# Sums of the attention in one trip, right-hand pieces by VectorE, an early opening of the gate's second half, and an own bank for its sixth product

## The chip, the cores and the metric

One core of one Trainium2 chip. The time is the device time of one execution in microseconds (us), the median of several runs. All arrays are fp32, and the matmuls run as three products of high and low parts (type fp32r): high x high, high x low and low x high.

## The reference

A block with two sublayers over 2048 tokens of width 640: windowed attention with 32 heads of 20, then a gated MLP in which a 2048x2048 matrix mixes tokens.

```python
x = A_x                                  # 2048 x 640
n = layernorm(x)
q, k, v = split(n @ wqkv)                # 32 heads of 20
p = softmax(q @ k.T * 20 ** -0.5, where 0 <= i - j < 256)
h = x + (p @ v) @ wo
z = gelu(layernorm(h) @ w_in)            # 2048 x 1728
z1, z2 = z[:, :864], layernorm(z[:, 864:])
g = w_sp @ z2 + b_sp[:, None]            # w_sp 2048 x 2048
h2 = h + (z1 * g) @ w_out
```

## The kernel before

*Stages.* Tokens are 16 tiles of 128. The stages follow one another, and TensorE works through nearly all of them: norms and the projections to q, k and v; the attention, a loop of some 130 steps `s`; the projection by `wo` (about 460 to 550 us); z1 (to 640); z2 of tiles 0 to 7, and of tiles 8 and 12 ahead of their turn (to 697); the gate's first half, eight row pairs over columns 0 to 1023 of w_sp (to 831); z2 of the other tiles (831 to 867); the gate's second half, with the last product and the output (867 to 1127). Each engine runs its instructions in one fixed order, and what stands ahead of an instruction on its engine is ahead of it in time.

*What sets the order.* Within the attention, `proj_early(s)` issues preparations of the projection at numbered steps, and SyncE's order is fixed by hand. Elsewhere a scheduler orders each engine by its own estimate of times, starting from the order in which the code issues. From z1 on the work is a list `steps`, each a product on TensorE and then the reading of its PSUM bank; `at(n, f)` issues a preparation at step n, `n0` is the first step of a pair.

*End of the attention.* `ot` is the unnormalised output of a head group, read out of its PSUM bank `pv` and stored to `o_d` in DRAM; row DH = 20 of it holds the softmax sums. `inverse_sums(c)` loads the sums of 512 tokens into `inv` (128x128), inverts them and stores them to `r_d`, from where `load_rs` spreads them over 128 partitions into the end of the buffer `m1`. `load_o(j)` loads two token tiles into m1 by five loads, `norm_o` multiplies by the inverse, `split_o` makes the high part (on VectorE where its second argument is True, otherwise on ScalarE) and the low part in `xb`, and `proj_o` multiplies by wo into `wo_ps`; then VectorE adds the residual `xh` and takes the statistics `mvc`.

*The gate.* For w_sp and z2 a pair of row tiles (p, p + 8) and a pair of z2 tiles are taken as 2x2 blocks, and seven products stand for the eight of a plain block product (Strassen's scheme in Winograd's form). They run in the order B11, T1, T2, B22, T3, B21, T4. Each has pieces of w_sp on the left (buffer `aw`, seven places of 1024 columns, high and low part; raw values in `fx`, one sum in `tmp1`) and pieces of z2 on the right (`zc[k]`, k = 0 to 3; in names ze0 to ze11 and zl0 to zl15 by 7k + product). A high part is a copy on ScalarE (`hi`, line 707), a low part or a block's sum is a subtraction (`lo`, `plus`, `minus`, line 701) by VectorE, or by GpSimd (POOL in the profile) where `eng` says so. Products share two banks of PSUM per pair: B11 and T1 open them, and each product's `post` reads its bank before a later one goes on in it.

*Rows and z2.* `row0` to `row3` are tiles of 128x864 that hold the results of a z2 pair or of a gate pair; a gate pair of the first half is stored to `g_d` and loaded back in the second half. `z2_pair` makes gelu, the norm and, by `right_blocks`, the pieces; a pair with `ahead` is stored to `z2_d`, and `z2_ready` loads it again at the end of the first half, splits it and fills zc[0]. `hn_d` holds the normed h. `win2_prep` is a generator, advanced once a step from z1 on, that loads the five 128x864 blocks of w_in's second half and splits them.

## Time and profile before

| what | value |
|---|---|
| time, median of 3 runs | 1132.14 us (1131.96 to 1132.17) |
| the profiled execution's own time | 1129.15 us |
| its span in the profile | 1127.4 us |
| mean granted TensorE clock | 0.994 |
| HBM traffic over the span | 154 GB/s |

In the rows of the profile PE is TensorE's matmuls, PEld its weight loads, DVE VectorE, ACT ScalarE, POOL GpSimd, SPq the queue of SyncE, which issues most DMAs. A row of the timeline reads: start in us, duration, engine, line, operation, out<-in by the program's names without their numbers, partitions x elements and type, count, and in brackets the idle time of the engine just ahead with what ended it. The time of a profiled execution lies a little off the median, since each execution has its own.

### The profile page before, as it was taken

How to read it: one execution, taken by the hardware profiler on the slowest of the kernel's cores; microseconds unless marked ns; L12 is line 12 of the kernel's file. 1: busy time of each engine (PE TensorE's matmuls, PEld its weight loads, DVE VectorE, ACT ScalarE, POOL GpSimd, SP SyncE). 2: the span in 40 equal slices, each digit the busy share in tenths (PEclk: the TensorE clock that was granted, in tenths of full speed). 3: DMA queues.
4: the chain of work that ended last, by engine and by line, in shares of the span. 5: the costliest groups of instructions: out<-in, count | busy, mean ns of one | idle time of the engine just before them, and what ended most of it. 6: DMA issues, size and time to landing. Idle time of an engine off the chain costs nothing.

```text
span 1127.4 us, 27668 instructions
## 1 busy us (share of the span) xinstructions
PE 1094.3 (97%) x10667; PEld 979.1 (87%) x10667; DVE 729.4 (65%) x2047; ACT 563.0 (50%) x1197; POOL 338.0 (30%) x470
## 2 busy tenths in 40 slices
PE   9999999999999999999999999999999899999998
PEld 7998877668877776799989999999988799999998
DVE  6541113889999998599567578545548965465542
ACT  4334333259999989435756567333336522122210
POOL 3114444457777768312120254000025000000000
PEclk9999999999999999899999999999999899999999
DMA  7212665656666653688645412343251554344322
GB/s 257 76 32 99 177 210 177 211 192 204 205 205 192 220 159 116 199 267 291 235 147 196 157 47 61 114 138 114 90 168 55 183 183 141 127 136 147 98 76 78
DMA packets 84580, 174.26 MB, mean 155 GB/s; under 512 B 11152, under 2 KB 47504, under 8 KB 80528
## 3 DMA queue, kind: packets, MB, share of 16 engines
q1 hardware_dynamic: 82144, 167.24, 46.2%
q10 hardware_dynamic: 2304, 5.24, 1.2%
q8 instruction: 84, 1.38, 0.5%
q14 instruction: 48, 0.39, 0.1%
HBM read 114.89 MB, written 58.75 MB: 154 GB/s over the span
## 4 chain that ended last, share of the span: by engine, by line
PE 74%; DMA 7%; DVE 6%; issue 4%; POOL 3%; ACT 3%; SPq 2%; POOLq 0%; DVEq 0%; ACTq 0%
PE g L1059 22%; PE out_ps L1098 8%; PE pv L419 6%; PE zb L947 5%; PE bank L325 5%; PE bank L391 5%; PE qk L509 2%; PE qk L511 2%; PE qk L510 2%; PE wo_ps L93 2%; PE zx L895 2%; PE zv L895 1%; POOL sg L528 1%; DMA qk_d<-sg 1%; PE zy L895 1%
## 5 line engine op out<-in xcount | busy, mean ns | idle before, releaser
L394 ACT ACTIVATE pt<-bank 128x384 f32<-128x384 f32 (+2 forms) x512 | 200.5, 495 | 12.6 <-PE bank L391 7.5
L1059 PE MATMUL g<-zl,aw 128*128 128x432 f32 x768 | 172.0, 360 | 5.1 <-ACT zl L707 4.5
L707 ACT ACTIVATE aw<-fx 128x512 fp32r<-128x512 f32 (+3 forms) x160 | 92.7, 594 | 166.5 <-PE g L1059 104.8
L337 DVE CUSTOM_DVE_ANT_0 junk<-bank,strip 128x288 bf16<-128x288 f32 x392 | 157.7, 454 | 4.4 <-PE bank L325 2.9
L1059 PEld LDWEIGHTS g<-zl,aw 128*128 128x128 f32 x768 | 144.2, 189 | 12.7 <-ACT zl L707 5.1
L1059 PE MATMUL g<-ze,aw 128*128 128x432 f32 x576 | 135.8, 364 | 4.2 <-DVE row L701 2.4
L419 PE MATMUL pv<-pt,v_sb 128*32 128x192 f32 (+3 forms) x1984 | 128.3, 322 | 1.7 <-POOL pt L399 0.6
L701 DVE TENSOR_TENSOR aw<-fx,aw 128x512 fp32r<-128x512 f32 (+3 forms) x152 | 104.9, 699 | 35.0 <-ACT aw L707 34.6
L1059 PEld LDWEIGHTS g<-ze,aw 128*128 128x128 f32 x576 | 108.0, 190 | 11.7 <-ACT aw L707 3.0
L391 PE MATMUL bank<-slot 123*32 123x288 bf16 (+5 forms) x1536 | 107.2, 280 | 1.1 <-ACT pt L394 0.6
L396 POOL TENSOR_SCALAR_AFFINE_SELECT pt<-pt 128x512 f32<-128x512 f32 x128 | 82.3, 643 | 51.7 <-ACT pt L394 50.7
L1098 PE MATMUL out_ps<-wout,y_sp 128*128 128x320 f32 (+1 forms) x630 | 96.2, 309 | 0.4 <-ACT y_sp L134 0.4
L947 PE MATMUL zb<-win,aw 128*128 128x432 f32 x480 | 95.5, 359 | 0.0
L1098 PEld LDWEIGHTS out_ps<-wout,y_sp 128*128 128x128 f32 (+1 forms) x630 | 94.1, 188 | 1.3 <-ACT y_sp L134 0.7
L947 PEld LDWEIGHTS zb<-win,aw 128*128 128x128 f32 x480 | 89.9, 188 | 5.0 <-ACT aw L707 0.4
L325 PE MATMUL bank<-slot 120*32 120x288 bf16 (+2 forms) x1264 | 88.8, 283 | 3.1 <-issue 2.1
L525 DVE TENSOR_TENSOR rest<-qk,sg 128x512 f32<-128x512 f32 x40 | 27.7, 692 | 86.1 <-ACT sg L523 86.1
L399 POOL TENSOR_SCALAR_AFFINE_SELECT pt<-pt 128x512 f32<-128x512 f32 x112 | 73.9, 660 | 0.0
L701 DVE TENSOR_TENSOR row<-g,row 128x432 f32<-128x432 f32 x80 | 48.0, 603 | 31.4 <-PE g L1059 27.3
L419 PEld LDWEIGHTS pv<-pt,v_sb 128*32 128x32 f32 x1984 | 60.6, 110 | 8.6 <-issue 2.4
L391 PEld LDWEIGHTS <-slot 123*32 123x32 bf16 x1536 | 53.6, 96 | 16.6 <-issue 5.4
L528 POOL TENSOR_TENSOR sg<-rest,sg 128x512 bf16<-128x512 f32 x40 | 46.6, 1164 | 69.6 <-ACT sg L527 57.3
(190 smaller groups left out, 2161.4 us busy)
## 6 DMA issues: line engine op xcount, KB each, us to landing
fx<-wsp_in SPq DMA_DIRECT2D x32, 512.0 KB
slot<-qk_d SPq DMA_DIRECT2D x72, 200.0 KB
qk_d<-sg SPq DMA_DIRECT2D x32, 384.0 KB
slot<-qk_d SPq DMA_DIRECT2D x72, 160.0 KB
fx<-hn_d SPq DMA_DIRECT2D x32, 320.0 KB
o_d<-ot SPq DMA_DIRECT2D x64, 128.0 KB
z_d<-row SPq DMA_DIRECT2D x18, 432.0 KB
g_d<-row SPq DMA_DIRECT2D x16, 432.0 KB
```

The source lines that it names most:

```text
L325: nc.tensor.matmul(ps[32 * j:32 * j + 32, :n], part(st, half, 120, 0, hh, q0, 32), part(st, half, 120, 1, hh, lo + skip * j, n), start=Tru ...
L337: nc.vector.tensor_tensor_reduce(out=junk[:, :n], in0=ps[:, :n], in1=keep, scale=1.0, scalar=NEG, op0=OP.add, op1=OP.max, accum_out=m_cols ...
L391: nc.tensor.matmul(ps[32 * i:32 * i + 32, b:e], part(st, half, 123, 1, hh, k0, 32), part(st, half, 123, 0, hh, kb * P + b, e - b), start=T ...
L394: nc.scalar.activation(pt[:, hh, :n], ps[:, :n], AF.Exp, scale=SCALE)
L396: nc.gpsimd.affine_select(out=pt[:, :, :P], in_=pt[:, :, :P], pattern=[[0, 4], [1, P]], base=0, channel_multiplier=-1, compare_op=OP.is_ge ...
L399: nc.gpsimd.affine_select(out=pt[:, :, 256:], in_=pt[:, :, 256:], pattern=[[0, 4], [-1, P]], base=-1, channel_multiplier=1, compare_op=OP. ...
L419: nc.tensor.matmul(ps[32 * hh:32 * hh + 32, a - 512 * c:b - 512 * c], v_sb[:, kb, v0:v0 + 32], pt[:, hh, a - kb * P:b - kb * P], start=fir ...
L701: (eng or nc.vector).tensor_tensor(out=out, in0=a, in1=b, op=op)
L707: nc.scalar.activation(out, a, AF.Copy)
L947: nc.tensor.matmul(b[0][:, :HF], a[t][:, x, kk], win2[0][:, y, kk, h * HF:(h + 1) * HF], start=kk + x + y == 0, stop=kk == KD - 1 and x == 1)
L1059: nc.tensor.matmul(ps, w[m][:, x, k], zc[k][m][:, y], start=start and k + x + y == 0, stop=stop and k == 3 and x == 1, skip_group_check=True)
L1098: nc.tensor.matmul(ps[j][:, :HD], src[:w, a, k, :], e1["wout"][:w, b, k, j * HD:(j + 1) * HD], start=(k == 0 and a + b == 0), stop=(k == K ...
```

## The change

- `load_o` gives three functions. `load_sums` loads the sums of the first two tiles straight from o_d, spread over 128 partitions, and VectorE inverts them in place (128x256). This serves tiles 0 and 1; the others use r_d as before. The loads begin at step 117 instead of 118, the norms and splits of tiles 0 and 1 run at steps 122 to 125 instead of 125 to 127, and the high part of tile 2 is made by VectorE.
- `win2_prep` subtracts on VectorE, with five steps instead of four between load and copy and behind the subtraction.
- `z2_pair` of pairs 13 and 14 (q > 12) makes its pieces with VectorE alone, as pair 15 did.
- `z2_ready` loads into two row tiles instead of places of `fx`, at n0 - 5 and n0 - 4 instead of n0 - 9 and n0 - 8, and its first pieces come one or two steps later.
- `gate_pair`, second half: sums by VectorE in the first pair too (`p or c`). The first pair (`alone`) loads w_sp at n0 - 23 and makes the pieces of B11, T1, T2 at n0 - 17 to n0 - 14; B21 has its own place in aw and its own bank, opened by itself, and its pieces are made at n0 - 4 and n0 - 3; the second pair's preparations shift by one step. The order in which the code issues the products stays; the scheduler may put B21 elsewhere.
- The rows of the second half and the raw tile of w_out change names to match.

```diff
@@ load_o
-        for k in range(KD):
-            nc.sync.dma_start(ot[:, k], o_d[:, 4 * k:4 * k + 4, t])
+        def load_tiles():
+            for k in range(KD):
+                nc.sync.dma_start(ot[:, k], o_d[:, 4 * k:4 * k + 4, t])
...
+        def load_sums():
+            load_rs(o_d[:, DH, t], 32 * S)
+            return lambda: nc.vector.reciprocal(out=rs, in_=rs)
+
+        return load_tiles, load_rs, load_sums
@@ proj_early
-        if s == 118:
-            mem["rs"] = [load_o(0)]
+        if s == 117:
+            tiles, _, sums = load_o(0)
+            mem["invert"] = sums()
+            tiles()
         if s == 121:
-            mem["rs"][0]()
-            load_o(1)()
+            for f in load_o(1)[:2]:
+                f()
+            mem["invert"]()
+        if s == 122:
+            norm_o(0, nc.vector)
+        if s == 123:
+            split_o(0, True)
+        if s == 124:
+            norm_o(1, nc.vector)
         if s == 125:
-            norm_o(0, nc.vector)
+            split_o(1, True)
         if s == 126:
-            split_o(0, True)
...
         if s == 127:
...
-            norm_o(1, nc.vector)
-            split_o(1, True)
@@ win2_prep
-            for _ in range(4):
+            for _ in range(5):
...
-            minus(win2[0][:, 1, k], raw, win2[0][:, 0, k].bitcast(F32), nc.gpsimd)
-            for _ in range(4):
+            minus(win2[0][:, 1, k], raw, win2[0][:, 0, k].bitcast(F32))
+            for _ in range(5):
@@ z2_pair
-        f = right_blocks(lambda: zc[k], *blocks, nc.vector if k == 3 else nc.gpsimd)
+        f = right_blocks(lambda: zc[k], *blocks, nc.vector if k == 3 or q > 12 else nc.gpsimd)
@@ z2_ready
-        z = [view(fx, 2048 + t * FH, FH) for t in range(2)]
+        z = [row(), row()]
...
-            at(n0 - 9 + t, lambda t=t: nc.sync.dma_start(z[t], z2_d[t]))
-        for n, g in zip((-5, -4, -3, -1, 0, 0, 0), f):
+            at(n0 - 5 + t, lambda t=t: nc.sync.dma_start(z[t], z2_d[t]))
+        for n, g in zip((-3, -3, -2, -1, 0, 0, 0), f):
@@ gate_pair
+        alone = p == 0 and c == 1
+        if alone:
+            w[B21] = two(view(aw, 4608, 2, 4, P))
+            w[T3] = [view(aw, o, 4, P) for o in (4096, 5632)]
...
-        eng = nc.vector if p else nc.gpsimd
+        eng = nc.vector if p or c else nc.gpsimd
...
+        if p == 1 and c == 1:
+            preps[4:7] = [(-2, lambda: lo(T2, a11)), (-1, lambda: (hi(T3, a21), hi(B21, a12))),
+                          (0, lambda: (lo(T3, a21), s4(), hi(T4, a22)))]
...
-        at(n0 - 11 if p != 1 else n0 - 10, load)
+        if alone:
+            preps = [(-17, lambda: hi(B11, a11)), (-16, lambda: (lo(B11, a11), s13(), hi(T1, s1))),
+                     (-15, lambda: (s2(), lo(T1, s1), hi(T2, a11))), (-14, lambda: lo(T2, a11)),
+                     (-4, lambda: hi(B21, a12)), (-3, lambda: lo(B21, a12)), (-2, lambda: minus(a12, a12, a11)),
+                     (0, lambda: (hi(T3, a21), hi(T4, a22))), (1, lambda: (hi(B22, a12), lo(T3, a21))),
+                     (2, lambda: (lo(B22, a12), lo(T4, a22)))]
+        at(n0 - (10 if p == 1 else 23 if alone else 11), load)
...
-            if m in (B11, T1):
-                gbank[p, half] = bank("a", f"g{c}_{p}_{half}")
+            if m in (B11, T1) or m == B21 and alone:
+                gbank[p, half] = bank("b" if m == B21 else "a", f"g{c}_{p}_{half}_{m}")
@@ the loop of the projection
-            split_o(i + 1, False)
+            split_o(i + 1, i == 1)
```

In the orders below, the numbers behind the names only tell buffers apart. On VectorE at the end of the attention, before (`inv` and `r_d` carry the inverted sums, `ot7` and `pv7` the last head group, xb0 and xb1 the parts for the projection):

```order
L373 RECIPROCAL inv0_8951<-inv0_8951 128x128
L435 COPY ot7_1_0_9267<-pv7_1_9087 128x256
L435 COPY ot7_1_1_9270<-pv7_1_9087 128x256
L158 TENSOR_TENSOR m1_8946<-m1_8946 128x5x128
L164 CAST xb0_96<-m1_8946 128x640
L167 TENSOR_TENSOR xb0_96<-m1_8946,xb0_96 128x640
L158 TENSOR_TENSOR m1_8946<-m1_8946 128x5x128 x2
L373 RECIPROCAL inv1_8952<-inv1_8952 128x128
L158 TENSOR_TENSOR m1_8946<-m1_8946 128x5x128
L167 TENSOR_TENSOR xb1_97<-m1_8946,xb0_96 128x640
L164 CAST xb1_97<-m1_8946 128x640
```

and after:

```order
L384 RECIPROCAL inv0_8951<-inv0_8951 128x128
L446 COPY ot7_1_0_9268<-pv7_1_9087 128x256
L446 COPY ot7_1_1_9271<-pv7_1_9087 128x256
L157 RECIPROCAL m1_8946<-m1_8946 128x256
L163 TENSOR_TENSOR m1_8946<-m1_8946 128x5x128
L169 CAST xb0_96<-m1_8946 128x640
L172 TENSOR_TENSOR xb0_96<-m1_8946,xb0_96 128x640
L163 TENSOR_TENSOR m1_8946<-m1_8946 128x5x128
L169 CAST xb1_97<-m1_8946 128x640
L163 TENSOR_TENSOR m1_8946<-m1_8946 128x5x128 x2
L172 TENSOR_TENSOR xb1_97<-m1_8946,xb1_97 128x640
L384 RECIPROCAL inv1_8952<-inv1_8952 128x128
```

The 128x256 reciprocal in m1 is new; the norm, high and low parts of tile 0 and the high part of tile 1 (`CAST xb1`) now stand ahead of the norms of tiles 2 and 3 (`x2`), and the low part of tile 1 behind them. On SyncE, at the loads that feed these, before:

```order
L436 DMA o_d_66<-ot7_0_0_9124 128x256
L436 DMA o_d_66<-ot7_0_1_9127 128x256
L370 DMA inv0_8951<-o_d_66 128x1x128
L146 DMA m1_8946<-o_d_66 128x1x256 x5
L374 DMA r_d_67<-inv0_8951 32x4x128
L436 DMA o_d_66<-ot7_1_0_9267 128x256
L436 DMA o_d_66<-ot7_1_1_9270 128x256
L152 DMA m1_8946<-r_d_67 128x1x256
L146 DMA m1_8946<-o_d_66 128x1x256 x5
```

and after:

```order
L447 DMA o_d_66<-ot7_0_0_9124 128x256
L447 DMA o_d_66<-ot7_0_1_9127 128x256
L153 DMA m1_8946<-o_d_66 128x1x256
L147 DMA m1_8946<-o_d_66 128x1x256 x5
L381 DMA inv0_8951<-o_d_66 128x1x128
L385 DMA r_d_67<-inv0_8951 32x4x128
L447 DMA o_d_66<-ot7_1_0_9268 128x256
L447 DMA o_d_66<-ot7_1_1_9271 128x256
L147 DMA m1_8946<-o_d_66 128x1x256 x5
L153 DMA m1_8946<-r_d_67 128x1x256
```

The load of the sums takes the place of `inv`'s, which goes behind the five tile loads, and r_d's first load goes. On VectorE at the end of the gate's first half (`g0_7` is the last pair, row0 and row1 its result, `ze` the pieces of z2), before:

```order
L701 TENSOR_TENSOR ze4_10556<-fx_9613,ze4_10556 128x432
L701 TENSOR_TENSOR fx_9613<-fx_9613 128x512
L701 TENSOR_TENSOR row1_9608<-g0_7_0_12604,row1_9608 128x432
L701 TENSOR_TENSOR aw_9612<-fx_9613,aw_9612 128x512
L701 TENSOR_TENSOR ze3_10555<-fx_9613,ze3_10555 128x432
L701 TENSOR_TENSOR row0_9607<-g0_7_1_12621,row0_9607 128x432
L701 TENSOR_TENSOR aw_9612<-fx_9613,aw_9612 128x640
L701 TENSOR_TENSOR ze5_10557<-fx_9613,ze5_10557 128x432
```

and after:

```order
L712 TENSOR_TENSOR row1_9609<-g0_7_0_0_12605,row1_9609 128x432
L712 TENSOR_TENSOR aw_9613<-fx_9614,aw_9613 128x512
L712 TENSOR_TENSOR ze0_10553<-row2_9610,ze0_10553 128x432
L712 TENSOR_TENSOR row2_9610<-row2_9610 128x432
L712 TENSOR_TENSOR ze3_10556<-row3_9611,ze3_10556 128x432
L712 TENSOR_TENSOR row2_9610<-row3_9611,row2_9610 128x432
L712 TENSOR_TENSOR row0_9608<-g0_7_1_1_12622,row0_9608 128x432
L712 TENSOR_TENSOR aw_9613<-fx_9614,aw_9613 128x640
```

Before, one piece (`ze3`) stands between the readings of g0_7_0 into row1 and of g0_7_1 into row0; after, four rows that read the loaded row2 and row3 do. On SyncE the loads of z2 there, before:

```order
L1072 DMA g_d_71<-row0_9607 128x864
L999 DMA fx_9613<-z2_d_73 128x864 x2
L1073 DMA g_d_71<-row3_9610 128x864
L956 DMA fx_9613<-hn_d_70 128x640
L1072 DMA g_d_71<-row2_9609 128x864
L956 DMA fx_9613<-hn_d_70 128x640 x2
L1073 DMA g_d_71<-row1_9608 128x864
```

and after:

```order
L1097 DMA g_d_71<-row3_9611 128x864
L967 DMA fx_9614<-hn_d_70 128x640
L1010 DMA row3_9611<-z2_d_73 128x864
L1096 DMA g_d_71<-row2_9610 128x864
L1010 DMA row2_9610<-z2_d_73 128x864
L967 DMA fx_9614<-hn_d_70 128x640 x2
L1097 DMA g_d_71<-row1_9609 128x864
```

The loads from z2_d went behind the last pairs' stores, and row2's load directly follows the store out of row2. On TensorE at the opening of the gate's second half (`g1_0_0` and `g1_0_1` are the banks of the first pair), before:

```order
L1059 MATMUL g1_0_0_13073<-ze0_10552,aw_9612 128x432 x3
L1059 MATMUL g1_0_0_13073<-ze7_10559,aw_9612 128x432 x3
L1059 MATMUL g1_0_0_13073<-zl2_9593,aw_9612 128x432 x3
L1059 MATMUL g1_0_1_13100<-ze1_10553,aw_9612 128x432 x3
L1059 MATMUL g1_0_1_13100<-ze8_10560,aw_9612 128x432 x3
L1059 MATMUL g1_0_1_13100<-zl3_9594,aw_9612 128x432 x3
L1059 MATMUL g1_0_0_13073<-zl9_9600,aw_9612 128x432 x3
L1059 MATMUL g1_1_0_13216<-ze0_10552,aw_9612 128x432 x2
```

and after:

```order
L1083 MATMUL g1_0_0_0_13075<-ze0_10553,aw_9613 128x432 x3
L1083 MATMUL g1_0_0_0_13075<-ze7_10560,aw_9613 128x432 x3
L1083 MATMUL g1_0_0_0_13075<-zl2_9594,aw_9613 128x432 x3
L1083 MATMUL g1_0_1_1_13100<-ze1_10554,aw_9613 128x432 x3
L1083 MATMUL g1_0_1_1_13100<-ze8_10561,aw_9613 128x432 x3
L1083 MATMUL g1_0_1_1_13100<-zl3_9595,aw_9613 128x432 x3
L1083 MATMUL g1_0_1_5_13174<-ze5_10558,aw_9613 128x432 x3
L1083 MATMUL g1_0_1_5_13174<-zl0_9592,aw_9613 128x432 x3
L1083 MATMUL g1_0_1_5_13174<-zl7_9599,aw_9613 128x432 x3
L1083 MATMUL g1_0_0_0_13075<-zl9_9601,aw_9613 128x432 x3
L1083 MATMUL g1_0_1_5_13174<-zl14_9606,aw_9613 128x432
```

Nine matmuls of B21 (ze5, zl0, zl7, bank g1_0_1_5) now stand ahead of the first matmul with zl9, a piece made from the last z2 pair.

More of the change, by code (lines that the diff above doesn't have):

```diff
@@ L144, in load_o, with load_rs @@
         ot, rs = m1(j % 2 * 2 * D, KD, 2 * P), m1(6 * D + j % 2 * 2 * P, 2 * P)
-        for k in range(KD):
-            nc.sync.dma_start(ot[:, k], o_d[:, 4 * k:4 * k + 4, t])
+        def load_tiles():
+            for k in range(KD):
+                nc.sync.dma_start(ot[:, k], o_d[:, 4 * k:4 * k + 4, t])
         for i in range(2):
             ots[2 * j + i] = (ot[:, :, i * P:(i + 1) * P], rs[:, i * P:(i + 1) * P])
-        def load_rs():
-            base = r_d[:, t]
-            nc.sync.dma_start(rs, bass.AP(tensor=base.tensor, offset=base.offset, ap=[[S, H], [0, 4], [1, 2 * P]]))
-        return load_rs
+        def load_rs(base=r_d[:, t], step=S):
+            nc.sync.dma_start(rs, bass.AP(tensor=base.tensor, offset=base.offset, ap=[[step, H], [0, 4], [1, 2 * P]]))
+        def load_sums():
+            load_rs(o_d[:, DH, t], 32 * S)
+            return lambda: nc.vector.reciprocal(out=rs, in_=rs)
+        return load_tiles, load_rs, load_sums
     def norm_o(i, eng):
@@ L1013, in gate_pair @@
         s1 = view(tmp1, 0, 4, P)
-        w = [view(aw, m * 1024, 2, 4, P) for m in range(7)]
+        w = [two(view(aw, m * 1024, 2, 4, P)) for m in range(7)]
+        alone = p == 0 and c == 1
+        if alone:
+            w[B21] = two(view(aw, 4608, 2, 4, P))
+            w[T3] = [view(aw, o, 4, P) for o in (4096, 5632)]
         def load():
@@ L1018, in load @@
                 nc.sync.dma_start(view(fx, f0 + o, 8, P), wsp[t, :, 8 * c:8 * c + 8, :])
-        eng = nc.vector if p else nc.gpsimd
+        eng = nc.vector if p or c else nc.gpsimd
         def hi(m, raw):
-            copy(w[m][:, 0], raw)
+            copy(w[m][0], raw)
         def lo(m, raw):
-            minus(w[m][:, 1], raw, w[m][:, 0].bitcast(F32))
+            minus(w[m][1], raw, w[m][0].bitcast(F32))
         def s13():
@@ L1058, in prod @@
                 for x, y in ((0, 0), (0, 1), (1, 0)):
-                    nc.tensor.matmul(ps, w[m][:, x, k], zc[k][m][:, y], start=start and k + x + y == 0,
+                    nc.tensor.matmul(ps, w[m][x][:, k], zc[k][m][:, y], start=start and k + x + y == 0,
                                      stop=stop and k == 3 and x == 1, skip_group_check=True)
@@ L1118, in final_half @@
             nc.sync.dma_start(out[tile_of(n) * P:(tile_of(n) + 1) * P, c], ht[:, c])
-    gate_rows = (rows[n] for n in [0, 1] + [2, 0, 1] * 5)
+    gate_rows = (rows[n] for n in [2, 3] + [0, 2, 1] * 5)
     def second_gate(p):
@@ L1162, in wout_raw @@
             def wout_raw(k):
-                return e1["h"][0 if k < 4 else 1]
+                return e1["h"][0] if k < 4 else rows[1][:, :D]
             def load_wout(k):
@@ L1198, in block_kernel @@
         if 1 < i + 1 < NT:
-            split_o(i + 1, False)
+            split_o(i + 1, i == 1)
         if i % 2 == 0 and i + 4 < NT:
-            load_o(i // 2 + 2)()
+            for f in load_o(i // 2 + 2)[:2]:
+                f()
         if i + 2 < NT:
```

## Prediction

> **What bounds the kernel now.** I read the page's head first, then the waits of TensorE, then tables of windows around each wait, and last the timelines of the engines that end the waits.
>
> ```profile
> span 1127.4 us, 27668 instructions
> PE 1094.3 (97%) x10667; PEld 979.1 (87%) x10667; DVE 729.4 (65%) x2047; ACT 563.0 (50%) x1197; POOL 338.0 (30%) x470
> ```
>
> TensorE is busy for 97% of the span, so 33 us are all that edits of the other engines can win, plus what a lowered clock adds. The change removes no matmul. The question is which pieces of those 33 us it touches. The columns below are window, length, then busy time with count for PE, PEld, DVE, ACT and POOL, and the granted clock.
>
> ```profile
> 465.00:468.70 3.70, 1.59 (x21) 0.91 (x20) 3.61 (x6) 1.23 (x3) 0.59 (x1) 0.92 0.77 214
> 468.70:474.80 6.10, 6.03 (x22) 6.03 (x23) 2.85 (x8) 2.28 (x4) 0.55 (x1) 0.50 0.93 315
> 831.50:867.30 35.80, 35.76 (x182) 33.63 (x181) 25.46 (x46) 19.42 (x34) 18.06 (x15) 1.00 0.35 112
> 867.00:875.50 8.50, 3.98 (x21) 3.44 (x19) 8.29 (x14) 6.17 (x12) 5.81 (x6) 0.93 0.22 67
> 875.50:881.20 5.70, 4.79 (x11) 3.55 (x12) 4.63 (x10) 4.18 (x7) 0.46 (x1) 0.51 0.97 345
> 876.00:906.00 30.00, 27.75 (x127) 24.54 (x127) 28.06 (x49) 14.84 (x25) 0.00 (x0) 0.91 0.56 177
> ```
>
> Two places lose time. At the end of the attention TensorE idles 3.70 - 1.59 = 2.1 us, and then runs 6.03 us at clock 0.50, where full clock would need 3.0: together 5.1 us. At the opening of the gate's second half it idles 8.50 - 3.98 = 4.5 us and then 30.00 - 27.75 = 2.25 us, and 4.79 busy us run at clock 0.51, which costs 2.35 more: 9.1 us.
>
> **The change, part by part.**
>
> *End of the attention.* Here is who holds whom now.
>
> ```profile
> 449.71 0.95 DVE L373 RECIPROCAL inv<-inv 128x128 f32<-128x128 f32 x1 [1.31 <-DMA inv<-o_d]
> 450.58 0.69 DVE L435 COPY ot<-pv 128x256 f32<-128x256 f32 x2
> 462.00 1.56 DVE L158 TENSOR_TENSOR m<-m 128x640 f32<-128x640 f32 x2 [1.42 <-DMA m<-r_d]
> 466.19 0.81 DVE L164 CAST xb<-m 128x640 fp32r<-128x640 f32 x1
> 467.95 0.76 DVE L167 TENSOR_TENSOR xb<-m,xb 128x640 fp32r<-128x640 f32 x1
> 467.10 0.53 PE L93 MATMUL wo_ps<-xb,xb 128*128 128x320 f32 x2 [1.03 <-PE pv L419]
> 468.77 1.43 PE L93 MATMUL wo_ps<-xb,xb 128*128 128x320 f32 x4 [0.85 <-DVE xb L167]
> ```
>
> The second projection starts at 467.10, just after the high part of tile 1 (466.19 + 0.81 = 467.00; the row names another releaser, but the time fits this one), and waits again for the low part (467.95 + 0.76 = 468.71). Both come late because VectorE first waited for the inverted sums to travel out and back. The change loads the sums straight from o_d and inverts them in place. A 128x128 reciprocal takes 0.95; for 128x256 I take 1.75 (below: 0.95, above: 1.9). That lets tiles 0 and 1 be normalised before the queue's second trip. The cast of tile 1 then stands near 462 and its low part, which the new order puts behind the normalisation of tiles 2 and 3, near 466. The 5.1 us go.
>
> What is late next is the first trip itself, which still serves tiles 2 and 3 and is now queued behind six loads.
>
> ```profile
> 447.38 0.60 SPq L370 DMA_DIRECT2D inv<-o_d  x1
> 448.03 3.17 SPq L146 DMA_DIRECT2D m<-o_d  x5
> 447.38 2.31 DMA inv<-o_d
> 458.06 3.92 DMA m<-r_d
> 454.50 0.41 PE L419 MATMUL pv<-pt,v_sb 128*32 128x128 f32 x8
> 496.35 0.56 PE L93 MATMUL wo_ps<-xb 128*128 128x320 f32 x2 [1.51 <-DVE mvc L710]
> ```
>
> The sums take the slot at 447.38, the five tile loads follow, and inv is issued at 451.25 instead of 447.38. It lands 2.31 (as now) to 3.92 us later (as r_d does behind five loads), 453.6 to 455.2; I take 454.4. VectorE runs in order, so the reciprocal (0.87 to the next start) and then the two copies of the pv bank (0.69) end at 456.0, where they now end at 451.3. The bank is wanted by the matmul of 454.50 (the first with 128 columns after one of 256, so a new bank): a new wait of 1.5 us, 0.7 to 2.3. Behind that wait stand scores that ScalarE needs. The rest of the lead, 3.6 us, meets the wait of 1.51 at 496.35, which an accumulator bank ends when VectorE adds the residual. VectorE is there held by loads of SyncE, whose queue has as many issues as before. I estimate that release 2.0 us earlier, so 1.6 us are given back. Sum: -5.1 + 1.5 + 1.6 = -2.0 us; bounds -5.1 (nothing given back) and +1.0 (the new wait at its largest, and its clock lost as at 468.7, against a lead that is all used up). Tile 2's cast moves from ScalarE to VectorE (0.8 us), in idle time of VectorE that the earlier projection leaves, and frees the last exponentials of the attention: nothing by itself; uncovered, it costs its 0.8.
>
> *win2 by VectorE.*
>
> ```profile
> 580.52 2.05 POOL L701 TENSOR_TENSOR win<-fx,win 128x864 fp32r<-128x864 f32 x1 [4.76 <-ACT win L707]
> 580.78 2.08 DVE L701 TENSOR_TENSOR aw<-fx,aw 128x256 fp32r<-128x256 f32 x1 [1.44 <-ACT aw L707]
> 584.33 0.41 DVE L701 TENSOR_TENSOR aw<-fx,aw 128x256 fp32r<-128x256 f32 x1
> 585.84 1.82 PE L895 MATMUL zx<-zl,aw 128*128 128x432 f32 x8 [0.84 <-ACT row L707]
> ```
>
> While GpSimd subtracts (580.52 to 582.57), VectorE's 128x256 row takes 2.08 us instead of 0.41. The rows behind it free the bank for 585.84, whose wait is 0.84. Five such GpSimd rows become five VectorE rows of about 1.0 (twice the 0.52 from one 432-wide row's start to the next, 882.44 to 882.96 below); two steps more around each give its load more time. VectorE has room in this stage. I take -0.8, bounds -1.3 and +0.5.
>
> *End of the gate's first half: row tiles for z2.* The stored pair is now loaded into row2 and row3 instead of fx. row2 is still being stored when the load is due, so SyncE waits for the store to land, and VectorE has four rows that need this load ahead of the bank's evacuation.
>
> ```profile
> 820.96 0.32 SPq L1072 DMA_DIRECT2D g_d<-row  x1
> 471.93 3.44 DMA o_d<-ot
> 886.92 3.38 DMA row<-g_d
> 828.37 0.61 DVE L701 TENSOR_TENSOR row<-g,row 128x432 f32<-128x432 f32 x1 [0.56 <-PE g L1059]
> 829.03 0.86 PE L1059 MATMUL g<-ze,aw 128*128 128x432 f32 x3 [0.70 <-DVE row L701]
> ```
>
> Store issued 820.96, landed after some 3.44 (the row of another store, a smaller one) at 824.4; the load is of the size of the 3.38 row and lands at 827.8. Then one high part on ScalarE (0.56 as at 874.90 below) and four rows of VectorE at 0.52, with one further ScalarE pair between them, end near 830.5, and the evacuation (0.61, now at 828.37) ends at 831.1. The last product of the pair restarts that bank: it starts at 831.2 instead of 829.03, +2.2 us. This product still shares its bank here; the own bank is only for the second half's first pair. Queued behind on SyncE are three loads of hn, 1 us late; they are needed only after that product. Bounds: -0.7 (the load is in time and today's wait goes too) and +5.2 (2.2, and the 3.0 us that the half clock cost at 468.7). The idle time ahead of that product would be about 2.9 us. Above, 4.5 us of idle time were followed by a half clock, and 1.51 us were not. The Trainium skill ("TensorE: Matmul & The Clock Gate", What's actually happening) has the clock fall after an idle window of about 3.4 us, free-running, which this trace neither fixes nor contradicts; by that rule alone the clock stays and the sum stands, and if the window were met the sum would be 3 us less of a gain.
>
> *Opening of the second half.*
>
> ```profile
> 866.74 0.51 ACT L951 ACTIVATE row<-zb 128x432 f32<-128x432 f32 x1
> 869.56 1.95 DVE L701 TENSOR_TENSOR zl<-row,zl 128x432 fp32r<-128x432 f32 x2
> 871.07 1.39 POOL L701 TENSOR_TENSOR row<-row,row 128x432 f32<-128x432 f32 x1 [0.55 <-DVE zl L701]
> 874.90 0.56 ACT L707 ACTIVATE zl<-row 128x432 fp32r<-128x432 f32 x1
> 875.51 0.73 PE L1059 MATMUL g<-zl,aw 128*128 128x432 f32 x1 [4.54 <-ACT zl L707]
> 882.44 0.60 DVE L701 TENSOR_TENSOR row<-row,row 128x432 f32<-128x432 f32 x1
> 882.96 0.60 DVE L701 TENSOR_TENSOR zl<-row,zl 128x432 fp32r<-128x432 f32 x1
> ```
>
> The last zb matmul ends at 867.2. The first piece that depends on it is written at 874.90, 7.7 us later, after 18 matmuls (3.6 us) that were ready. Two things make it late. ScalarE reads out zb15_0_1 at 866.74 though TensorE had left it two products of 3 us earlier, since ScalarE runs in order behind rows that wait for GpSimd. And VectorE stretches beside GpSimd (two rows in 1.95 instead of 1.04).
>
> Of the change, three parts work here. Eight GpSimd subtractions become VectorE rows: 8 x 0.52 = 4.2 us more for VectorE. The pair's pieces B11, T1, T2 and their sums, with their wsp loads, move ahead into the first half's last pair (six VectorE rows, 0.60 each, where VectorE has idle time; if not covered, 3.6 us). And product B21 gets its own bank and moves ahead: nine more matmuls (9 x 0.197 = 1.8 us; 35.76 / 182 = 0.197 in the window of 831.50) are ready before the first late piece.
>
> Worked through the new order row by row from the start of zb13, with 0.52 per 432-wide VectorE row (0.60 per 512-wide one, an estimate by width) and 0.51 per ScalarE row: from the first statistics of the 13th pair to the value that releases the 15th's normalisation VectorE has 23 us of work in some 23.5, so it is about even with TensorE. The first late high part then stands 5.8 us after the last zb matmul, the ready work lasts 27 x 0.197 = 5.3. What is left of waits: 0.5 for that piece and 0.4 for its low part; 0.7 for the second pair's first piece, whose place in aw is free only after B11; 0.4 for its T1; 1.4 for the evacuation of T2, behind VectorE's pieces. 3.4 us, each too short for the clock by the row at 496.35. 9.1 - 3.4 = 5.7 us gained. Bounds: -9.1 (all goes) and +3.7 (first rival).
>
> The changed row tiles of the later pairs and wout's raw tile exchange names at equal distances: nothing, hidden by SyncE's prefetch; uncovered, one load of 3.38.
>
> **The sum.** -2.0 - 0.8 + 2.2 - 5.7 = -6.3 us. The profiled execution took 1129.15, so 1122.85; the runs' median, 1132.14, lies 2.99 above it, so 1125.8.
>
> **The rivals.**
> - *Slower: VectorE pays for z.* Window 831.5:867.3 has VectorE busy 25.46 of 35.8; it gains 4.2 us there and is nearly saturated in the 30 us after (28.06). If it comes out of zb15 4 us later than now, the first late piece stands at 12 us, TensorE idles 6.5, pays 2.4 for the clock, and waits some 4 us more for pieces: 12.8 in place of 9.1, +3.7, total +3.1, 1135.2. It decides from about 9.5 us on. Against it: the 18.06 us of GpSimd that stretch VectorE's rows mostly go.
> - *No change that shows: the z2 trip.* With a load of 5 us and a lost clock the end of the first half costs 2.2 + 1.6 + 3.0 = 6.8: total -1.7, 1130.4. For it: the idle time is near the one that lost the clock. Against it: the other rows at that hour carry little DMA.
> - *More: the loads are in time.* Nothing lost at the first half's end, the attention's lead of 3.6 kept, the opening down to 2 us of waits: -3.6 - 1.3 + 0 - 7.1 = -12.0, 1120.1.
>
> **How the numbers follow.** Forecast 0.57 (own range 1122.5 to 1129.5), more 0.13, no change 0.18, slower 0.12. A measurement of this kernel tells about 0.2% (2.3 us) from nothing, so faster 0.70, same 0.18, slower 0.12. The range 1119.5 to 1134.0 leaves out most of the slower case and half of the largest gain, 0.16.
>
> **What the profile after would show.** Right: the second projection starts without the 1.03 and 0.85, and no half clock follows; a new wait of about 1.5 on a pv matmul near 455; the wait at 829.03 grown to near 2.9; no wait over 1.5 us after zb15 and a clock near 1.0; no POOL row on win2 or on z tiles after the first half. Wrong: a wait of several us on the first zl piece; a half clock near 831; the projections after tile 6 as late as now; new waits in the first half where six more VectorE rows stand.

## The result and the profile after

The changed kernel takes 1125.98 us (median of 11 runs, 1122.33 to 1129.96) against 1132.17 for the kernel before (1128.27 to 1136.89, 11 runs). The ratio is 0.9944, 95% interval 0.9925 to 0.9963, that is 6.3 us less, 4.2 to 8.5. Forecast were 1125.8 and -6.3. The total was right, partly by luck: of its four terms two were too small by about two us and one by one, and the largest error, at the end of the attention, had the wrong sign; the errors partly cancel. Two executions ran in a slower state and count in no figure here: one of e9 (1519.28 us, granted clock 0.654) and one of the kernel before beside e1 to e4 (1330.1 us, 0.752).

The profiled execution of the changed kernel took 1128.62 us, 2.6 above its median, and that of the kernel before lay 3.0 below its own. So the two spans (1126.9 and 1127.4) tell almost nothing of the change. Stages do. The start of a stage is read from the views of single tiles, whose rows give the first and last start of their matmuls. In the changed kernel:

```profile
L366 PE MATMUL bank<-minus,m x16: 218/260/267, 226.8 to 439.8; 128*120 128x128 bf16 x8, 128*96 128x128 bf16 x8
L906 PE MATMUL zv<-zl,aw x120: 353/357/450, 556.0 to 640.6; 128*128 128x432 f32 x120
L1083 PE MATMUL g<-ze,aw x576: 353/360/562, 700.9 to 1105.9; 128*128 128x432 f32 x192
L958 PE MATMUL zb<-win,aw x480: 353/359/463, 638.3 to 874.5; 128*128 128x432 f32 x160
```

From the last maxima matmul (the transposing matmul with `minus` in the attention; 439.8, ahead of all that the change touches) to the first of z1 (zv) are 116.2 us; from there to the first gate matmul (g) 144.9; to the last z2 matmul (zb) 173.6; to the end of the span 252.4. The same four in the other traces (us; the experiments are told below):

| kernel | attention's end, projection | z1, first z2 | gate's first half, last z2 | gate's second half |
|---|---|---|---|---|
| before | 113.0 | 147.3 | 169.8 | 260.3 |
| changed | 116.2 | 144.9 | 173.6 | 252.4 |
| changed, second trace (e1) | 119.0 | 144.9 | 172.9 | 253.1 |
| e2, old attention end | 116.0 | 144.9 | 173.3 | 252.5 |
| e3, win2 by GpSimd | 118.6 | 147.3 | 171.7 | 253.0 |
| e4, own bank at first half's end | 117.4 | 144.9 | 168.6 | 253.6 |
| e5, no own bank | 118.9 | 144.9 | 173.0 | 258.1 |
| e6, z by GpSimd | 120.3 | 144.9 | 172.8 | 253.6 |
| e7, e4 with old attention end | 115.6 | 144.9 | 167.6 | 252.9 |
| e8, e4 with inv first | 114.3 | 144.8 | 167.9 | 253.3 |
| e9, before with the sums' part | 117.9 | 148.0 | 169.8 | 260.4 |
| e10, e9 with inv first | 112.6 | 145.6 | 169.7 | 260.6 |
| e11, e8 with x by GpSimd's queue | 111.7 | 145.5 | 167.5 | 253.0 |
| e12, e8 with z by GpSimd | 116.6 | 144.8 | 167.5 | 254.0 |

Where the code of a stage is the same, the last three columns repeat mostly within one us and, but for e10's second, within two; the first column spreads over some 3 to 4 us (the old end 113.0 to 116.0, the changed one 116.2 to 120.3, inv first 112.6 to 116.6), so no single trace tells 2 us there. e11's first column starts at a point that its own edit made late (below). TensorE's waits in the changed kernel, from its timeline:

```profile
458.47 0.42 PE L430 MATMUL pv<-pt,v_sb 128*32 128x128 f32 x8 [0.95 <-DVE ot L446]
485.83 0.53 PE L93 MATMUL wo_ps<-xb,xb 128*128 128x320 f32 x2 [2.37 <-DVE xh L1240]
526.28 1.33 PE L846 MATMUL ht_ps<-ident,m 128*128 128x128 f32 x5 [3.78 <-ACT m L1247]
834.92 1.15 PE L1083 MATMUL g<-ze,aw 128*128 128x432 f32 x3 [3.25 <-DVE row L712]
880.74 0.86 PE L1083 MATMUL g<-zl,aw 128*128 128x432 f32 x3 [0.18 <-DVE zl L712]
881.93 0.67 PE L1083 MATMUL g<-ze,aw 128*128 128x432 f32 x2 [0.32 <-ACT aw L718]
888.71 1.85 PE L1083 MATMUL g<-ze,aw 128*128 128x432 f32 x8 [0.76 <-ACT aw L718]
895.40 1.45 PE L1083 MATMUL g<-ze,aw 128*128 128x432 f32 x6 [1.10 <-DVE row L712]
```

The waits at the second projection and the 4.54 us behind the last z2 pair are gone. New are 0.95 on the pv bank, 2.37 on the residual and 3.78 on the normed h in the projection, and 3.25 at the end of the first half.

### The profile page after: what moved, and what is told of

Its sections match the earlier page's. It is cut to its first block, busy times and chain, and to the rows that moved or that the text cites. A ratio compares the mean times of both kernels' runs of the same rounds, so it can differ in the third digit from the quotient of the medians.

```text
span 1126.9 us, 27684 instructions
## 1 busy us (share of the span) xinstructions
PE 1094.8 (97%) x10667; PEld 980.9 (87%) x10667; DVE 733.7 (65%) x2065; ACT 565.5 (50%) x1196; POOL 308.0 (27%) x454
## 4 chain that ended last, share of the span: by engine, by line
PE 77%; DMA 6%; DVE 5%; issue 4%; POOL 3%; SPq 3%; ACT 2%; POOLq 0%; DVEq 0%; ACTq 0%
PE g L1083 22%; PE out_ps L1122 8%; PE zb L958 6%; PE pv L430 6%; PE bank L336 5%; PE bank L402 5%; PE zx L906 3%; PE zv L906 2%; PE qk L520 2%; PE qk L522 2%; PE qk L521 2%; PE wo_ps L93 2%; PE zy L906 2%; POOL sg L539 1%; PE zw L906 1%
## 5 line engine op out<-in xcount | busy, mean ns | idle before, releaser
L718 ACT ACTIVATE aw<-fx 128x512 fp32r<-128x512 f32 (+2 forms) x160 | 93.2, 595 | 175.1 <-PE g L1083 111.2
L712 DVE TENSOR_TENSOR aw<-fx,aw 128x512 fp32r<-128x512 f32 (+2 forms) x152 | 96.9, 646 | 32.2 <-ACT aw L718 30.9
L712 POOL TENSOR_TENSOR aw<-fx,aw 128x640 fp32r<-128x640 f32 x8 | 13.6, 1698 | 215.1 <-ACT aw L718 215.1
```

Source lines behind the costliest of these rows:

```text
L712: (eng or nc.vector).tensor_tensor(out=out, in0=a, in1=b, op=op)
L718: nc.scalar.activation(out, a, AF.Copy)
```

## The experiments

**e1: the changed kernel again.** No edit.

> The changed kernel once more, unaltered, for a second trace and as the one to compare with. Theory (the four terms of the prediction): 0.994 of the time before, and the first trace's clock losses are partly chance. The waits of TensorE in the projection stage of the first trace (2.37 us on the residual, 3.78 us on the normed h) and 3.25 us at the end of the gate's first half come from the order and should stand again within 1 us. Rival (the projection's waits are chance of DMA times): they shrink below 1 us and the stage from the first projection matmul to the first z1 matmul takes 3 us less than the 92 us of the first trace.

Ratio 0.9940 (0.9921 to 0.9960). The waits on pv, the residual, the normed h and at 834 stand again (1.37, 3.73, 3.92, 2.69): they belong to the order, and the rival falls. Their size is partly chance: the residual's is 1.4 longer than in the first trace, more than the 1 us expected.

**e2: the old end of the attention.**

In `load_o`, `proj_early` and the loop of the projection the old code stands again: the sums by way of `r_d`, the loads at steps 118 and 121, the norms at 125 to 127, tile 2's high part on ScalarE.

> The changed kernel with the end of the attention as before (sums by r_d, loads and norms at the old steps, tile 2's high part on ScalarE). Theory of the prediction: this part is worth -2.0 us, so this kernel is 2 us slower than the changed one. Rival, from the first trace (the gain of 5.1 us at the end of the attention is lost again within the projection: new waits of 0.95, 2.37 and 3.78 us and clock lost behind them): this kernel is 2 to 4 us faster than the changed one, and the projection stage is back to 90 us. If it is within 1 us, gain and loss cancel.

Ratio 0.9930 (0.9907 to 0.9954), median 1124.16. The kernel is not 2 us slower without this part; the 1.2 to 1.8 us by which it is faster can't be told from nothing here. Its trace shows why the 5.1 us at the old end were not all to be had. The clock stayed up this time, and TensorE met a new wait (the first row is a window, its columns as in the prediction, the last two the share of the DMA engines and GB/s):

```profile
474.00:480.00 6.00, 6.00 (x44) 5.99 (x43) 3.02 (x6) 1.48 (x2) 0.00 (x0) 1.00 0.82 262
476.98 1.56 DVE L158 TENSOR_TENSOR m<-m 128x640 f32<-128x640 f32 x2 [3.76 <-DMA inv<-o_d]
483.37 0.53 PE L93 MATMUL wo_ps<-xb,xb 128*128 128x320 f32 x2 [2.29 <-DVE xh L1228]
```

The second row is the norm of tiles 4 and 5, which waits for loads, and the residual that frees TensorE's bank stands behind it on VectorE. The old start of the projection is already early enough to run into that: what the clock lost in the profile before, TensorE loses here by waiting, and the stage takes 116.0 us against 113.0.

**e3: win2 by GpSimd again.**

```diff
-            minus(win2[0][:, 1, k], raw, win2[0][:, 0, k].bitcast(F32))
+            minus(win2[0][:, 1, k], raw, win2[0][:, 0, k].bitcast(F32), nc.gpsimd)
```

> The changed kernel with w_in's second half subtracted by GpSimd again, four steps each side. Theory: 0.8 us slower than the changed kernel, with the waits of 0.4 and 0.8 us on ScalarE's row back in the z1 stage. Rival from the first trace (z1 and first z2 stage, from the first z1 matmul to the first gate matmul, 144.9 us instead of 147.3): 2.4 us slower.

The steps around it are four again. Ratio 0.9955 (0.9935 to 0.9976); the stage is 147.3 instead of 144.9, and the two waits of the z1 stage are back:

```profile
584.84 0.86 PE L906 MATMUL zx<-zl,aw 128*128 128x432 f32 x3 [0.37 <-ACT row L718]
589.45 1.82 PE L906 MATMUL zx<-zl,aw 128*128 128x432 f32 x8 [0.83 <-ACT row L718]
```

The rival's 2.4 holds in the stage; the median of the times is 1.4 to 2.0 us above the changed kernel's two.

**e4: an own bank also at the end of the first half.**

```diff
-            if m in (B11, T1) or m == B21 and alone:
+            if m in (B11, T1) or m == B21 and (alone or p == 7 and c == 0):
```

> The changed kernel, and also the first half's last pair gives its sixth product an own bank (tag b). Theory (the 3.25 us wait at the end of the first half is the sixth product waiting for the read-out of its shared bank, which stands behind the pieces of the reloaded z2 row): the sixth product runs ahead, the wait goes, and what is late next is the high and low part of h for the 13th z2 pair, ready at 835.5 in the first trace where TensorE would be done at 834.0: about 1.5 us of waiting in place of 3.65, no clock lost: 2 to 4 us faster than the changed kernel. Rival (VectorE's rows behind the load hold all that follows): the same wait stands on the first matmul of the 13th pair, no gain within 1 us.

Ratio 0.9921 (0.9891 to 0.9951). The stage falls from 173 to 168.6 (167.5 to 167.9 in the four later traces with this bank). The median, 1123.28 us, is 2.1 to 2.7 us below the changed kernel's two, with intervals that overlap. All that is left of 3.65 us of waits (0.40 and 3.25) is this, on the first matmul of the 13th pair:

```profile
832.55 1.35 PE L1083 MATMUL g<-zl,aw 128*128 128x432 f32 x6
834.37 5.83 PE L958 MATMUL zb<-win,aw 128*128 128x432 f32 x27 [0.47 <-ACT aw L718]
```

So the wait was one for the shared bank, and the pieces behind the load are not needed there.

**e5: no own bank at the opening.**

```diff
-            if m in (B11, T1) or m == B21 and alone:
+            if m in (B11, T1):
```

> The changed kernel, but the sixth product B21 of the second half's first pair shares its bank again (its pieces stay where they are). Stage compared: from the last matmul of the z2 pairs to the end of the span, 252.4 and 253.1 us in the two traces of the changed kernel, 260.3 before. Theory (nine matmuls of 0.197 us cover the time until the first piece of the last z2 pair): 1.8 us longer, 254.5, as a wait of about 1.8 us on the first matmul with that piece. Rival (the pieces behind it are the limit, the waits only move): no change within 0.5. Second rival (the wait is long enough to lower the clock): 3 to 5 us longer.

Ratio 0.9998 (0.9973 to 1.0022): without the own bank the whole gain is gone. The stage is 258.1, 5.4 longer, not 1.8. The expected wait is there, but others follow:

```profile
877.28 0.47 PE L1083 MATMUL g<-zl,aw 128*128 128x432 f32 x1 [1.61 <-ACT zl L718]
879.11 0.66 PE L1083 MATMUL g<-ze,aw 128*128 128x432 f32 x2 [0.52 <-ACT aw L718]
886.21 0.47 PE L1083 MATMUL g<-zl,aw 128*128 128x432 f32 x1 [1.59 <-ACT zl L718]
887.14 1.98 PE L1083 MATMUL g<-ze,aw 128*128 128x432 f32 x6 [0.46 <-DVE row L712]
```

Those of 1.59 and 0.46 stand 9 us behind the first. Windows of equal length from the last z2 matmul on, of e5 and then of the changed kernel:

```profile
871.80:900.00 28.20, 23.61 (x105) 20.52 (x104) 23.21 (x46) 14.80 (x24) 1.09 (x2) 0.94 0.59 195
874.50:902.70 28.20, 25.83 (x127) 22.68 (x127) 25.45 (x50) 15.43 (x25) 1.10 (x2) 1.00 0.63 210
```

TensorE starts 22 matmuls fewer in e5, which at 0.197 us each are 4.3 of the 5.4 us: 2.2 us more of idle time, and some 1.7 because the clock fell to 0.54 for 3.70 us behind the second of the long waits (row in the last section). So the theory has the first wait, and the second rival is right that the clock is lost, though not behind that first wait. The remaining 1.1 us was not traced.

**e6: the z2 pieces by GpSimd again.**

```diff
-nc.vector if k == 3 or q > 12 else nc.gpsimd
+nc.vector if k == 3 else nc.gpsimd
```

> The changed kernel, but GpSimd makes the pieces of the z2 pairs 13 and 14 again, as before. Same stage, 252.7 us on average in the changed kernel. Theory (VectorE stretches beside GpSimd and ScalarE waits for GpSimd's rows, so the last pair's first piece comes 7.7 us after the last z2 matmul, as before, against 5.3 us of ready work): a wait of 2.4 us, 255 us, and up to 257.5 if the clock falls. Rival (VectorE pays for z: the 4.2 us that it saves here bring the pieces forward): no longer than 252.7, or up to 2 us shorter.

Ratio 0.9977 (0.9957 to 0.9998). The times are 3.7 us above the changed kernel's (median of its 21 executions in both runs), but the stage of the one trace, 253.6, only 0.9. The 255 of the theory isn't met. VectorE doesn't pay for z, so the rival falls; where the other 2.8 us lie isn't settled.

**e7 and e8: two ways to mend the attention's end.** Both have e4's bank. e7 has the old end; e8 the sums in one trip, with this:

```diff
         if s == 117:
-            tiles, _, sums = load_o(0)
+            mem["tiles"], _, sums = load_o(0)
             mem["invert"] = sums()
-            tiles()
+        if s == 118:
+            mem["tiles"]()
```

> The own bank also at the first half's end, and the end of the attention as before the change. Theory now (the sums' part costs about 1 to 3 us and the own bank at the first half's end gains 2 to 4.7): 3 to 6 us below the changed kernel, near 1121. Stages: from the last transposing matmul of the attention's maxima to the first z1 matmul 113 to 116 us (116 to 119 with the sums' part), and 168.6 us from the first gate matmul to the last z2 one. Rival (the sums' part gains 2.0 as predicted and other losses only hide it): 1125.

> The own bank at the first half's end, the sums in one trip, but SyncE issues the load of the other sums (inv) ahead of the five tile loads instead of behind them. Theory A (the part loses because inv behind the tiles makes VectorE's two copies of the pv bank late, 0.8 to 1.4 us of wait, and holds SyncE until the reciprocal, which delays all later loads): the wait on pv goes, and the time from the last maxima matmul to the first z1 matmul falls from 116.2 to 119.0 to about 114.5. Theory B (the projection behind tile 3 is paced by the row of loads on SyncE, one more than before, whatever the order at its start): the wait on pv goes, a wait of 2 to 4 us on the residual near the fourth projection stays, and that time stays at 116 or more.

e7: 0.9902 (0.9871 to 0.9932), 1121.15 us. e8: 0.9873 (0.9845 to 0.9902), 1117.68 us, the fastest of all by its median; the two intervals overlap, so this pair alone doesn't show that the part now gains (e9 and e10 do). SyncE's queue shows what one step in its order does, first in the changed kernel:

```profile
449.74 0.60 SPq L153 DMA_DIRECT2D m<-o_d  x1
450.39 3.18 SPq L147 DMA_DIRECT2D m<-o_d  x5
453.62 1.47 SPq L381 DMA_DIRECT2D inv<-o_d  x1
457.75 0.58 SPq L385 DMA_DIRECT2D r_d<-inv  x1
...
464.20 0.60 SPq L153 DMA_DIRECT2D m<-r_d  x1
...
476.93 0.60 SPq L153 DMA_DIRECT2D m<-r_d  x1
```

and in e8:

```profile
445.60 0.60 SPq L153 DMA_DIRECT2D m<-o_d  x1
446.30 0.56 SPq L382 DMA_DIRECT2D inv<-o_d  x1
446.91 3.18 SPq L147 DMA_DIRECT2D m<-o_d  x5
450.13 0.91 SPq L386 DMA_DIRECT2D r_d<-inv  x1
...
455.38 1.66 SPq L153 DMA_DIRECT2D m<-r_d  x1
...
467.53 0.51 SPq L153 DMA_DIRECT2D m<-r_d  x1
```

Counted from the load of the sums, the store of the inverse is issued 8.0 us later in the changed kernel (457.75 - 449.74), since it waits for a reciprocal whose load went behind five others; 4.5 in e8. All of SyncE's later loads stand behind that store: r_d for tiles 2 and 3 at 14.5 against 9.8, for tiles 4 and 5 at 27.2 against 21.9 (in the kernel before, counted from its load of inv, 10.7 and 26.5). The wait on pv is gone too, and the stage takes 114.3. Theory A holds; B holds in part, since a wait of 3.36 us on the residual, at 494, stays in e8. The stage alone carries little: e12, with the same order, took 116.6.

**e9 and e10: the attention's end alone**, on the kernel before, as changed and with inv first.

> The kernel before with only the attention's end changed (sums in one trip, earlier norms and splits, tile 2's high part by VectorE; inv behind the tile loads). Theory of the prediction: 2.0 us faster than before, 0.998. Theory now (the lead is given back at waits for loads that SyncE issues later, and a wait on the pv bank is added): from the last maxima matmul to the first z1 matmul 118 us (113 to 116 in the three traces with the old end), 1 to 3 us slower than before, 1.001 to 1.003.

> The same, with inv issued ahead of the five tile loads. Theory now: the same stretch near 114, so 3 to 4 us faster than with inv behind, and between 0 and 3 us faster than before (0.997 to 1.000). Rival (the fall from 1123.3 to 1117.7 between the kernels with the own bank at the first half's end came from elsewhere): as with inv behind.

e9: 1.0022 (1.0003 to 1.0042), 2.4 us slower by the mean, 1.7 by the median. e10: 0.9966 (0.9943 to 0.9989), 3.4 us of median faster, a little more than expected. The intervals are apart, so the order of one load decides whether the part loses or gains. SyncE's loads of r_d come as in the pair above: 14.3 and 27.6 us behind the load of the sums in e9, 10.0 and 21.5 in e10. In e10 the z1 stage, too, is 1.7 us shorter than before (145.6), without a wait over 0.2 us, though GpSimd still makes win2; in e9 it is 148.0. In this one trace, then, the waits there hang on when the stage is reached.

**e11: x and w_in's raw half through GpSimd's queue**, on e8.

```diff
-        nc.sync.dma_start(hs[i], x[i * P:(i + 1) * P, :])
+        nc.gpsimd.dma_start(hs[i], x[i * P:(i + 1) * P, :])
...
-        nc.sync.dma_start(mem["wraw"][:, b], src[r:r + P])
+        nc.gpsimd.dma_start(mem["wraw"][:, b], src[r:r + P])
```

> The fastest version so far (own bank at the first half's end, inv ahead of the tile loads), and the loads of x's tiles and of w_in's raw first half are issued from GpSimd's queue instead of SyncE's (some 20 issues of 0.33 to 0.55 us). Theory (behind tile 3 the projection is paced by SyncE's row of issues): the wait of 3.4 us on the residual near the sixth projection shrinks, the stretch from the last maxima matmul to the first z1 matmul falls from 114.3 to about 111, and the time by 2 to 3 us to 1115. Rival (the transfers themselves or VectorE's waits for the round trip over r_d and hn pace it): no change within 1 us; GpSimd's rows for the norms could come later.

The stage reads 111.7, 2.6 less, and the longest wait in the projection 2.30 instead of 3.36. But the time doesn't follow: 0.9882 (0.9851 to 0.9913), which isn't told from e8. The stage is counted from the last maxima matmul, which came 8 us later than in e8 (444.1 against 435.8), and the trace shows that the edit did some 4.5 of them; the rest lies further ahead and stays open. The new issues stand among GpSimd's own rows, which make the values for that matmul:

```profile
437.50 0.48 POOL L359 TENSOR_TENSOR mr<-mcol,m 128x32 f32<-128x32 f32 x1
...
443.83 0.24 POOL L361 TENSOR_TENSOR m<-mr,m 128x32 bf16<-128x32 f32 x1
444.13 0.34 PE L367 MATMUL bank<-minus,m 128*96 128x128 bf16 x1 [5.11 <-POOL m L361]
```

Between the two GpSimd rows lie 6.33 us here, with issues of x and w_in from 437.93 to 442.63, and 1.86 in e8 (433.68 to 435.54); TensorE waits 5.11 us where it waited 0.64. So the issues were moved to an engine whose rows the attention's end waits for, and whether SyncE's issues pace the projection is not shown.

**e12: z by GpSimd, on e8.**

> The fastest version so far with the pieces of the z2 pairs 13 and 14 by GpSimd again. In the changed kernel this cost 3.7 us in the times, but only 0.9 us of it stood in the stage of one trace. Theory (the loss lies in the opening of the second half, and in some executions the clock falls there): 2 to 4 us slower than the version without it, and the stage from the last z2 matmul to the end 254 to 257 us against 253.3. Rival (chance): within 1 us.

0.9884 (0.9853 to 0.9916), 1.4 us above e8 in the median, stage 254.0 instead of 253.3. The intervals overlap: inconclusive.

## Why the prediction was right, and where it was wrong

*End of the attention: wrong, -2.0 forecast (-5.1 to +1.0), +2.4 measured alone (e9; 0.3 to 4.8 by its interval, 1.7 by the median).* The step that failed is "VectorE is there held by loads of SyncE, whose queue has as many issues as before. I estimate that release 2.0 us earlier". The count was right, the times were not. The prediction priced inv's delay for VectorE and the pv bank (1.5 forecast, 0.95 and 1.37 measured), but not for SyncE itself, which issues in order and stands at the store of the inverse. The loads behind came later than before the change instead of earlier (r_d for tiles 2 and 3 at 14.5 against 10.7), all of the lead was given back, and more. With that order mended the same part gains (e10). The 5.1 us of lost time that the term began with weren't all to be had either: e2 ran the old end without the half clock, and its stage was no shorter. Nor do the stated parts of the upper bound make +1.0: with the wait at 2.3, the 2.8 left of the lead given back and 3.0 for the clock it is -5.1 + 2.3 + 2.8 + 3.0 = +3.0, which would have held the result.

*win2: right in sign, mis-sized, -0.8 (-1.3 to +0.5) against -2.4 in the stage (e3).* The mechanism was as told. VectorE's 128x256 rows went back to 0.42, and win2's own rows take 1.06 against the estimate of 1.0:

```profile
L712 DVE TENSOR_TENSOR win<-fx,win x5: 1058/1058/1060, 563.5 to 587.9; 128x864 fp32r<-128x864 f32 x5
568.28 0.42 DVE L712 TENSOR_TENSOR aw<-fx,aw 128x256 fp32r<-128x256 f32 x1 [1.26 <-ACT aw L718]
```

The Trainium skill ("SBUF — State Buffer", Who interferes with whom) has that a VectorE instruction with two SBUF inputs contends with a GpSimd instruction that reads SBUF. The traces agree: 2.08 beside such a row, 0.42 without. The size was wrong because the waits were read from the idle column (0.42 + 0.84 = 1.26). A matmul stands in it with 0.36 us, but one follows another every 0.197, so a wait costs some 0.16 more than its idle time. Counted from start to start in the trace before, the 30 matmuls from 579.46 to 587.50 take 8.04 us where 30 x 0.197 make 5.9, so 2.1 us are lost there:

```profile
579.46 1.33 PE L895 MATMUL zv<-zl,aw 128*128 128x432 f32 x6
581.22 0.86 PE L895 MATMUL zx<-zl,aw 128*128 128x432 f32 x3 [0.42 <-ACT row L707]
...
587.50 1.93 PE L895 MATMUL zy<-zl,aw 128*128 128x432 f32 x9
```

In e10, with GpSimd's rows, the stage was only 0.7 longer than the changed kernel's, so the 2.4 holds for the arrival times of e3 and not for all.

*z2's trip: right, +2.2 against +3.1* (172.9 on average over the six traces with that code, and 169.8 before). Each link stands in the changed kernel's timelines of SyncE, ScalarE and VectorE:

```profile
824.59 0.32 SPq L1096 DMA_DIRECT2D g_d<-row  x1
827.48 0.32 SPq L1010 DMA_DIRECT2D row<-z_d  x1
831.47 0.56 ACT L718 ACTIVATE ze<-row 128x432 fp32r<-128x432 f32 x1 [4.85 <-DMA row<-z_d]
834.27 0.60 DVE L712 TENSOR_TENSOR row<-g,row 128x432 f32<-128x432 f32 x1
```

Store to load 2.9 (3.44 assumed), load to first piece 4.0 (3.38), piece to read-out 2.8. The wait is 3.25 (2.9 forecast). What came on top is the clock (0.57 over 4.00 us, some 1.7 us), which the sum had left out and the bounds held; in e3, where it stayed up, the stage is 171.7, +1.9. The sum left it out on a reading of "4.5 us of idle time" against "1.51 us", but the prediction's own first rows had a nearer case: 2.1 us of idle time in 465.00:468.70, and 0.50 in the window behind it. No run takes this part of the change out alone; that the wait is the one for the shared bank is shown by e4.

*Opening of the second half: right, mis-sized, -5.7 against -7.5* (252.75 on average over e1, e2, e3 and the first trace, and 260.3). The first late high part was forecast 5.8 us after the last z2 matmul and came 4.6 us after it, at 879.50 (that matmul starts at 874.5 and ends near 874.9):

```profile
879.50 1.46 ACT L718 ACTIVATE zl<-row 128x432 fp32r<-128x432 f32 x3
```

The waits there are 2.4 us (0.18, 0.32, 0.76, 1.10) instead of 3.4. Its parts were mis-weighed: the own bank alone is worth 5.4 (e5), not 1.8, of which some 1.7 are the clock that is lost without it. The early pieces and the sums by VectorE were not taken out alone.

*The sum.* +2.4 - 2.4 + 3.1 - 7.5 = -4.4 us by the single measurements, against -6.3 (4.2 to 8.5) for the whole. The difference is within the interval of the first term alone. The errors were +4.4, -1.6, +0.9 and -1.8; that they cancel to +1.9, within the noise, is luck, and the agreement of the total says nothing for the term of the attention.

*The rivals.* "VectorE pays for z" is refuted by e6 and by the first late piece. "The loads are in time" didn't come in the changed kernel; e8, with both losses mended, is 2.4 us below its 1120.1. "No change, the z2 trip" had the lost clock right, but not the size of the gain around it. Two of the prediction's signs of being wrong did come: a half clock behind the wait at 834.92, and projections no earlier than before (stage 116.2 and 119.0 against 113.0).

## What to carry to other kernels

A load that is moved behind others on an in-order queue delays not only who reads it but every later issue of that queue, if one of them waits for what is made from it: follow the queue to the next store that depends on it. Issues moved to another engine's queue stand ahead of that engine's own rows (e11). Idle time at the start of a stage is a gain only if the stage is not paced by something else; look for the wait that would take its place. A bank of its own for one product of a chain can be worth more than faster pieces, since the product can then stand wherever there is time to fill. A total that agrees does not confirm its terms: measure them one by one.

## What the runs showed of the hardware

The half clock doesn't follow from the length of a wait alone. In the changed kernel TensorE's clock was 0.52 behind the wait of 2.37 us and 0.57 behind that of 3.25; in e2 it stayed at 1.00 behind 2.29; in e3 it stayed at 1.00 behind 2.85, while in e1 it fell to 0.61 behind 2.69 at the same place. Windows right behind these waits (the clock is the third number from the end), first of the changed kernel:

```profile
487.50:490.70 3.20, 3.20 (x14) 3.20 (x14) 3.20 (x8) 1.74 (x3) 0.00 (x0) 0.52 0.71 230
835.00:839.00 4.00, 4.00 (x13) 3.68 (x14) 2.73 (x6) 2.29 (x5) 0.00 (x0) 0.57 0.28 84
```

of e2, of e3 and of e1:

```profile
483.40:487.50 4.10, 4.10 (x28) 4.10 (x29) 4.10 (x9) 1.31 (x2) 0.55 (x1) 1.00 0.81 261
```

```profile
834.60:838.50 3.90, 3.78 (x18) 3.28 (x19) 3.90 (x7) 2.44 (x5) 0.34 (x1) 1.00 0.30 84
```

```profile
834.70:838.50 3.80, 3.80 (x12) 3.53 (x13) 2.99 (x6) 2.49 (x5) 0.00 (x0) 0.61 0.32 88
```

The Trainium skill ("TensorE: Matmul & The Clock Gate", What's actually happening) gives a free-running window of about 3.4 us. That the same place falls in one run and not in another agrees with free-running; that waits of 2.37 and 2.69 us were enough does not agree with a whole window of 3.4 us idle. Nor need the idle time be one wait. In e5 2.54 us of it within 4.60 us left the clock at 1.00, and 2.05 us within 2.80 us were followed by 0.54:

```profile
875.60:880.20 4.60, 2.06 (x7) 0.98 (x7) 2.94 (x6) 3.91 (x8) 0.00 (x0) 1.00 1.00 395
884.50:887.30 2.80, 0.75 (x3) 0.35 (x3) 1.66 (x4) 2.33 (x5) 0.00 (x0) 1.00 0.00 0
887.70:891.40 3.70, 3.70 (x13) 3.40 (x12) 3.13 (x5) 0.74 (x1) 0.00 (x0) 0.54 0.87 273
```

So from about 2 us of idle time close together on, the lost clock belongs into the sum as a chance, and not only into the bounds.
